# Batch 7's seven products in another order, its u and tail in three rounds, and a tail matrix padded to 128 columns

## The chip, the cores and the metric

The kernel runs on one core of one Trainium2 chip. The metric is the device time of one execution in microseconds (us), the median over the runs shown. TensorE is called PE in the profile, VectorE DVE, ScalarE ACT, GpSimd POOL, and SyncE, which issues most DMAs, SP.

## The reference

Inputs are `q`, `k`, `v` of 8 batches x 8 heads x 576 positions x 64, and four matrices. Each batch passes through a linear attention and then through a mixer:

```python
kv = einsum('bhsf,bhfd->...', phi(k), v)      # phi: relu, times cos and sin of the position
x  = (phi(q) @ kv) / (phi(q) @ z + 1e-6)      # heads side by side: 576 x 512 per batch
h  = x^T @ U @ V                              # U 576 x 32, V 32 x 576
u  = x + h^T
out = u + relu(u @ w_ch1) @ w_ch2             # 512 x 2048 and 2048 x 512
```

## The kernel before, in words

**Tiling.** The 576 positions of a batch are 4 chunks of 128 and a tail of 64. The tails of two batches (2 pr and 2 pr + 1) share one tile of 128 partitions, so there are 8 main parts and 4 paired tails. All products run in bf16 with fp32 sums in PSUM, which has 8 banks: g0, g1, g2, T, o0, o1, and X, which is two banks allocated as one tile.

**The stages of a batch.** k and q are scaled (`k_prep`, `q_prep`), `kv_unit` makes kv, `x_unit` makes x, `A_unit` makes A = (x^T U)^T. `u_mm` (L468) multiplies V by A for the four groups `j` of 128 columns: each is a matmul with only 32 rows of contraction, placed on rows 32 j of the array, once for each of the 4 chunks. `u_add` (L481, DVE) adds x. `u_tail` (L488) does the same for the paired tails: for each j and for each of the two batches i one matmul whose weights `V_tl` have 32 rows and 64 columns, placed at rows 32 j and columns 64 i; the add is at L504. `utr_dma` transposes u by a DMA. `g1_main` (L569) is the first mixer product for the first six batches. For the paired tails it is `g1_tail` (L709). `half_part` (L862) is the second mixer product from batch 2 on, by seven products of half size in place of eight; eight matmuls with 256 columns for each part.

**Batches 6 and 7** also use seven products instead of eight for the first mixer matrix. `g1_cross(b, p, i)` (L651), i from 1 to 7, is a product of two matmuls for block pair p of 0 to 7. Product 1 opens the accumulator X, 6, 7 and 4 are added to it one after the other; product 2 is Y, which lies in the same bank as X; product 5 opens Z in another bank and 3 is added to it. Between these, `g1_join` (L682) reads the partial sums: `P1`, `U2` (copies of X by ACT) and `P5` (a copy of Z by ACT), `C11` (DVE, P1 + Y), `C22` (DVE, P5 + X, and then ACT's relu), `C12` (DVE, U2 + Z; ACT's relu of X, L688; DVE's relu, L698). For batch 7, X and Y lie in g0 and Z in g1 for even p, in g2 and T for odd p.

**The order of the work** is written out by hand. `slots` is a list of main steps; `todo` hangs further work behind a slot (`put`), in the order in which it was put. Every engine executes its instructions in the order in which the program issues them, and waits where a semaphore says so. In the last stage before the end, the slots of batch 7's groups alternate with the 14 half parts of batch 6 (`beside_g`): a group of p is products 1 and 2 of p and 7 of p-1 (`opened`, `third`), then a half part, then products 6 and 5 of p, 3 and 4 of p-1 (`second`, `closed`), then a half part.

`attention_plan` (L1000) sets the slots of u and tails. For batch 7 (w = 189, a_at = 14): `u_mm` of j = 0, 1, 2 behind slot 205, of j = 3 behind 208; `u_tail` of j = 0, 1, 2 behind 212, of j = 3 behind 214. These fall in batch 6's section, whose slots hold `g1_cross` and `g1_join` of batch 6 and the half parts of batch 5. There DVE also makes `w1_sum(4, 0)` (L613, L629), put behind slot 211 by the loop at L1442. `four_banks` (L457) allocates X anew for each of the four steps.

Of the kernel before, what the change touches and what calls it, by code (L numbers as in the profile page):

```python
# [17 lines left out]
def kernel(  # L18
# [27 lines left out]
    def tail(b):  # L46
        lo = TS * (b % 2)
        return slice(lo, lo + TS)
# [78 lines left out]
    def cast(eng, o, i):  # L127
        if eng is nc.scalar:
            nc.scalar.activation(out=o, in_=i, func=AF.Copy, bias=0.0, scale=1.0)  # L129
        else:  # L130
            eng.tensor_copy(out=o, in_=i)  # L131
# [83 lines left out]
    x_tl = const.tile([P, DM], BF16)  # L215
    U_bf = const.tile([P, 6, R], BF16)
    V_bf = const.tile([P, 4, P], BF16)
    V_tl = const.tile([P, TS], BF16)
    A_sb = [const.tile([P, P], BF16, name=f"A_sb{i}") for i in range(4)]
    v_tl = const.tile([P, H, E], BF16)  # L220
    V_.memset(v_tl[:, :, D:E], 1.0)
# [53 lines left out]

    def spread_evac(eng):
        cast(eng, V_bf, v_ps[0].rearrange("r (c p) -> r c p", c=4))
        cast(eng, V_tl, v_ps[1][:, 0:TS])


    k_p, q_p, q_pT, kv_sb, x_bf = {}, {}, {}, {}, {}
# [157 lines left out]
    def A_of(b):  # L439
        return A_sb[b % 4]  # L440
# [27 lines left out]
    def u_mm(b, *spare, js=range(4)):  # L468
        if b not in u_bf:
            u_bf[b] = pool.tile([P, 4, 4, P], BF16, tag="u_bf", bufs=3, name="u_bf")  # L470
        va.setdefault(b, {}).update(zip(js, four_banks(*spare)))
        for c in range(4):
            for j in js:
                rows = slice(j * R, j * R + R)
                nc.tensor.matmul(  # L475
                    out=va[b][j][:, c * P : c * P + P], lhsT=V_bf[rows, c, :],
                    rhs=A_of(b)[rows, :], start=(c == 0), stop=(c == 3),
                    tile_position=(j * R, 0),
                )
# [8 lines left out]
    def u_tail(pr, *spare, js=range(4)):  # L488
        if pr not in u_tl:
            u_tl[pr] = pool.tile(  # L490
                [P, DM], BF16, tag="k_p" if pr == 3 else "u_tl", bufs=1, name="u_tl"
            )
        vt = dict(zip(js, four_banks(*spare)))
        for i in range(2):
            for j in js:
                rows = slice(j * R, j * R + R)
                nc.tensor.matmul(
                    out=vt[j][tail(i), 0:P], lhsT=V_tl[rows, :],
                    rhs=A_of(2 * pr + i)[rows, :], start=True, stop=True,
                    tile_position=(j * R, i * TS),  # L500
                )
        for j in js:
            ns = slice(j * P, j * P + P)
            nc.vector.tensor_tensor(  # L504
                out=u_tl[pr][:, ns], in0=x_tl[:, ns], in1=vt[j][:, 0:P], op=ALU.add
            )

    def uT_alloc(b):
        if b not in uT:
# [100 lines left out]
    def diff(o, x, y, op=ALU.subtract):  # L610
        V_.tensor_tensor(out=o, in0=x, in1=y, op=op)  # L611
# [70 lines left out]
    def g1_join(b, p, i):  # L682

        w, lo, hi = cross[b, p], slice(0, 256), slice(256, 512)
        top, low = hid[b][:, p, :], hid[b][:, p + 8, :]

        def relu(o, x):
            nc.scalar.activation(out=o, in_=x, func=AF.Relu, bias=0.0, scale=1.0)  # L688

        if i == "C11":  # L690
            diff(top[:, lo], w["P1"], w["Y"], ALU.add)
        elif i == "C22":
            diff(low[:, hi], w["P5"], w["X"], ALU.add)
            relu(low[:, hi], low[:, hi])
        elif i == "C12":
            diff(top[:, hi], w["U2"], w["Z"], ALU.add)
            relu(low[:, lo], w["X"])
            V_.tensor_scalar(out=top, in0=top, scalar1=0.0, scalar2=None, op0=ALU.max)  # L698
        else:
            if (b, "kept") not in cross:  # L700
                cross[b, "kept"] = pool.tile(
                    [P, 2, 3, 256], FP32, tag="q_pT" if b == B - 1 else "q_p", bufs=1,
                    name="kept",
                )
            n = ("P1", "U2", "P5").index(i)
            w[i] = cross[b, "kept"][:, p % 2, n]
            cast(A_, w[i], w["Z" if i == "P5" else "X"])
# [292 lines left out]
    def attention_plan(b):  # L1000

        plan = []
        if b < 4:
            w, f_at, q_eng, k_eng, qtr, lo = PLAN[b]
        else:
            w, q_at, k_at, qtr, lo = PLAN[b]

        def put(at, f, *a, tag=False):
            if tag:
                a = a + spare(w + at)  # L1010
            plan.append((w + at, lambda: f(b, *a)))

        for n, c in enumerate(QORD):
            if b > 3:
                put(q_at[0] + q_at[1] * n, q_prep, c, q_at[2:])
                put(k_at[0] + k_at[1] * n, k_prep, c, k_at[2:])
                put(k_at[0] + (3 * n) // 2, v_prep, 0, H, (c,), (G_,))
                continue
            if b == 3:
                q_eng, k_eng = V_ if n == 3 else A_, A_ if n < 3 else None  # L1020
                put((-12, -11, -10, -7, -3)[n], q_prep, c, (q_eng, q_eng))
                put(n - 9 if n < 3 else -5, k_prep, c, (A_, k_eng))
                if n > 2:
                    put(2 * n - 12, k_prep, c, (None, V_))
                put(-4 if n > 2 else -6, v_prep, 0, H, (c,), (A_ if n > 2 else G_,))
                continue
            put(f_at + ((n - 1) % 5 if b == 2 else n), q_prep, c, (q_eng, q_eng))
            put(f_at + 6 + n, k_prep, c, (k_eng, k_eng))
            put((-6, -2, -1, -5, -5)[n], v_prep, 0, H, (c,), (V_ if n > 2 else A_,))
        for n, (c0, c1) in enumerate(((4, 5), (0, 2), (2, 4))):  # L1030
            at = qtr[n] if b > 4 else 1 if b == 3 and n == 2 else qtr + 2 * n
            put(at, qtr_dma, c0, c1)
        plan.append((w + (b == 2), lambda: kv_unit(b, 0, *spare(w), A_ if b > 2 else V_)))
        plan.append((w + 2, lambda: kv_unit(b, 1, *spare(w + 2), A_ if b > 2 else V_)))
        for n, c in enumerate(ORD):
            if b > 3:
                put((3 if b == B - 1 else 4) + 2 * n, x_unit, c, "X", 1)
            elif n % 2:
                put(9 if (b, n) == (3, 3) else 4 + (3 * n) // 2, x_two, c, tag=True)
            else:  # L1040
                put(4 + (3 * n) // 2, x_unit, c, "X", 1)
        a_at = 15 - b if b < 4 else 14
        if b == B - 1:
            put(a_at, A_unit, "s", 1, A_)
        else:
            put(a_at, A_unit, tag=True)
        odd = b % 2 == 1


        def two(at):  # L1050
            return [T1, ("s", 1)] if at >= 88 else [spare(at)] * 2

        if b == B - 1:
            plan.append((w + a_at + 2, lambda: u_mm(b, ("s", 1), js=(0, 1, 2))))
            plan.append((w + a_at + 5, lambda: u_mm(b, js=(3,))))
        else:
            plan.append((w + a_at + 2, lambda: u_mm(b, *two(w + a_at + 2))))
        for j in range(4):
            put(a_at + 2 + j + (2 if b > 4 and j > 1 else 0), u_add, j)
        put(a_at + 3, utr_dma, 0, 2)  # L1060
        put(a_at + (7 if b > 4 else 5), utr_dma, 2, 4)
        if odd:
            if b == B - 1:
                plan.append((w + a_at + 9, lambda: u_tail(b // 2, ("s", 1), js=(0, 1, 2))))
                plan.append((w + a_at + 11, lambda: u_tail(b // 2, js=(3,))))
            else:
                plan.append((w + a_at + 9, lambda: u_tail(b // 2, *two(w + a_at + 9))))
            put(a_at + (11 if b == B - 1 else 10), utr_dma, 4, 5)
        for at, t in zip(lo, loads(b + 1) if lo else ()):
            plan.append((w + at, t))  # L1070
        return plan
# [325 lines left out]
        g1_join(b, p, "P1")  # L1397
        g1_join(b, p, "C11")

    def second(b, p):  # L1400
        g1_cross(b, p, 6)
        g1_cross(b, p, 5)
        g1_join(b, p, "U2")
        g1_join(b, p, "P5")

    def sixth(b, p):
        g1_cross(b, p, 6)
        g1_join(b, p, "U2")
# [5 lines left out]
    def third(b, p):  # L1414
        g1_cross(b, p, 7)
        g1_join(b, p, "C22")

    def closed(b, p):
        g1_cross(b, p, 3)
        g1_cross(b, p, 4)  # L1420
        g1_join(b, p, "C12")

    def crossed(*steps):
        def go():
            for f, b, p in steps:
                f(b, p)

        return go
# [44 lines left out]
    sums(b6, 0, (at, at + 1, at + 6))  # L1473
    sums(b6, 1, (at + 13, at + 15, at + 19))

    def group(p, first, then):
        return crossed(*([(first, b7, p)] if p < 8 else []), *([(then, b7, p - 1)] if p else []))

    groups = [
        group(p, *fs) for p in range(9) for fs in ((opened, third), (second, closed))  # L1480
    ]
    def tail_cross(j):
        if j % 3 == 0:
            t = ps.tile([P, 2, 512], FP32, tag="X", bufs=1, name="gt_ps")[:, 0, :]
# [89 lines left out]
```

## Time and profile before

| what | value |
|---|---|
| runs | 293.47, 294.00, 294.44 us; median 294.0 us |
| the profiled execution | 294.23 us, its span 292.4 us (1.8 us lie around the span) |
| PE clock granted, mean | 0.997 |
| PE busy | 287.0 us, 98% of the span, 2944 matmuls |
| DVE, ACT, POOL busy | 206.7, 169.3, 56.4 us |
| PE matmul of 256 columns, start to start | 0.109 us (0.87 us for 8) |
| stretch 226 to 270 us (batch 7) | PE busy 44.0, DVE 31.8, ACT 26.1 us |

Matmuls are pipelined: a row of the timeline with eight of them shows 1.04 us, but the next matmul can start 0.87 us after the first. So a wait of PE shorter than the pipeline does not show as idle time. It is read from starts: eight matmuls that begin at t end their issue at t + 0.87, and where the next row of PE starts later, that is what it lost.

### The profile page before, as it was taken

Reading aid. Unit: us, or ns where it says so; the run is one execution under the profiler, and the core shown is the slowest. Engines: PE = TensorE matmul, PEld = TensorE weight load, DVE = VectorE, ACT = ScalarE, POOL = GpSimd, SP = SyncE. Lnnn points to the kernel's source line nnn. Section 1 sums busy time; section 2 is a strip of 40 time slices with the busy share of each in tenths; the row PEclk is TensorE's granted clock in tenths of the full one; section 3 lists DMA queues with packets and bytes.
Section 4 is the critical chain, followed back from the end, with each engine's and each line's share of the span. In section 5 each row is a group of like instructions: output and inputs, shape, how many; then the busy total and the mean of one; then the engine's idle time right before and its main releaser. Section 6 shows DMA issues by size and latency. Waiting matters only on the chain.

```text
span 292.4 us, 7343 instructions
## 1 busy us (share of the span) xinstructions
PE 287.0 (98%) x2944; PEld 194.7 (67%) x2944; DVE 206.7 (71%) x503; ACT 169.3 (58%) x353; POOL 56.4 (19%) x92
## 2 busy tenths in 40 slices
PE   8999999999999999999999999999999999999994
PEld 3785564447645545676767666766777888889883
DVE  5968856396876687657547794669968886765773
ACT  2955752177791767578836855497744555567210
POOL 6430500000020002300400501032101223303330
PEclk9999999999999999999999999999999999999998
DMA  7999999999998999999789929992901864336023
GB/s 223 305 254 251 268 151 211 211 331 214 335 196 160 293 242 231 230 328 275 147 216 259 280 66 247 251 302 60 246 4 29 103 143 110 54 92 143 4 103 116
DMA packets 95174, 56.18 MB, mean 192 GB/s; under 512 B 58692, under 2 KB 91844, under 8 KB 95140
## 3 DMA queue, kind: packets, MB, share of 16 engines
q1 hardware_dynamic: 84420, 43.94, 61.6%
q0 software_dynamic: 10528, 11.57, 19.5%
q8 instruction: 23, 0.38, 0.6%
q10 hardware_dynamic: 192, 0.20, 0.2%
q14 instruction: 11, 0.09, 0.2%
HBM read 36.86 MB, written 9.44 MB: 158 GB/s over the span
## 4 chain that ended last, share of the span: by engine, by line
PE 98%; DVE 1%; issue 0%; DVEq 0%
PE g_ps L579 30%; PE h_ps L891 27%; PE o_ps L759 10%; PE c_ps L676 7%; PE gt_ps L719 5%; PE w_ps L234 3%; PE kv_ps L347 3%; PE x_ps L422 3%; PE a_ps L445 1%; PE h_ps L759 1%; PE g_ps L596 1%; PE va_ps L475 1%; PE t_ps L377 1%; PE t_ps L365 1%; PE z_ps L1236 1%; PE kv_ps L1132 0%
## 5 line engine op out<-in xcount | busy, mean ns | idle before, releaser
L579 PE MATMUL g_ps<-uT,w_bf 128*128 128x512 bf16 x402 | 97.3, 379 | 0.0
L588 ACT ACTIVATE hid<-g_ps 128x512 bf16<-128x512 f32 x104 | 61.1, 599 | 57.1 <-PE g_ps L579 56.3
L579 PEld LDWEIGHTS <-w_bf 128*128 128x128 bf16 x402 | 37.5, 98 | 34.4
L891 PEld LDWEIGHTS <-hid 128*128 128x128 bf16 x480 | 45.6, 98 | 9.7
L891 PE MATMUL h_ps<-w_bf,hid 128*128 128x256 bf16 x288 | 37.1, 273 | 0.0
L759 PE MATMUL o_ps<-w_bf,hid 128*128 128x512 bf16 x128 | 30.1, 379 | 0.0
L891 PE MATMUL h_ps<-w_s,S 128*128 128x256 bf16 x208 | 26.5, 272 | 0.0
L131 POOL CAST v_ext<-vst 128x512 bf16<-128x512 f32 (+1 forms) x23 | 14.9, 676 | 59.0 <-DMA vst<-in_v_dram 30.4
L891 PE MATMUL h_ps<-w_s,hid 128*128 128x256 bf16 x192 | 24.9, 273 | 0.0
L847 DVE TENSOR_TENSOR o_sb<-o_sb,h_ps 128x256 f32<-128x256 f32 (+1 forms) x36 | 15.5, 432 | 12.2 <-PE h_ps L891 9.6
L891 PEld LDWEIGHTS <-S 128*128 128x128 bf16 x208 | 20.1, 98 | 4.4
L950 POOL DMA_DIRECT2D out_dram<-o_sb x16 | 9.9, 619 | 65.8 <-DVE o_sb L847 51.4
L483 DVE TENSOR_TENSOR u_bf<-x_bf,va_ps 128x512 bf16<-128x512 bf16 x27 | 17.6, 680 | 6.5 <-PE va_ps L475 2.8
L611 DVE TENSOR_TENSOR hid<-kept,c_ps 128x256 bf16<-128x256 f32 x36 | 14.2, 417 | 10.0 <-ACT kept L129 7.1
L847 DVE TENSOR_TENSOR o_sb<-u_bf,h_ps 128x256 f32<-128x256 bf16 x28 | 11.7, 417 | 13.5 <-PE h_ps L891 13.4
L759 PEld LDWEIGHTS <-hid 128*128 128x128 bf16 x128 | 11.5, 98 | 12.2
L949 POOL DMA_DIRECT2D o_sb<-u_bf x8 | 10.4, 1303 | 32.0 <-DVE rec L413 15.6
L719 PE MATMUL gt_ps<-uT_tl,w_bf 128*128 128x128 bf16 x256 | 16.2, 219 | 0.0
L129 ACT ACTIVATE kept<-c_ps 128x256 f32<-128x256 f32 x36 | 12.5, 380 | 5.9 <-PE c_ps L676 5.6
L432 DVE TENSOR_TENSOR x_bf<-x_ps,rec 128x512 bf16<-128x512 f32 x22 | 15.2, 691 | 0.8
L719 PEld LDWEIGHTS <-w_bf 128*128 128x128 bf16 x256 | 15.1, 98 | 0.7
L306 ACT ACTIVATE k_p<-kst,cosw 128x512 bf16<-128x512 f32 x20 | 14.2, 713 | 0.1
(189 smaller groups left out, 456.6 us busy)
## 6 DMA issues: line engine op xcount, KB each, us to landing
qst<-in_q_dram SPq DMA_DIRECT2D x14, 512.0 KB, 6.2
kst<-in_k_dram SPq DMA_DIRECT2D x14, 512.0 KB, 6.8
vst<-in_v_dram SPq DMA_DIRECT2D x12, 512.0 KB, 6.8
out_dram<-o_sb POOLq DMA_DIRECT2D x19, 256.0 KB, 4.2
out_dram<-o_sb SPq DMA_DIRECT2D x16, 256.0 KB, 2.6
w_bf<-in_moe_w_ch_dram POOLq DMA_DIRECT2D x7, 512.0 KB, 12.3
o_sb<-u_bf POOLq DMA_DIRECT2D x8, 256.0 KB, 3.7
qst<-in_q_dram SPq DMA_DIRECT2D x2, 640.0 KB, 13.5
```

The lines of the kernel that those rows point to most:

```text
L131: eng.tensor_copy(out=o, in_=i)
L306: nc.scalar.activation(out=o, in_=i, func=AF.Relu, bias=0.0, scale=w)
L432: nc.vector.tensor_tensor(out=x_of(b, c, rows).rearrange("p (g i d) -> p g i d", g=2, d=D), in0=view[:, :, :, 0:D], in1=rec[rows].unsqueez ...
L483: nc.vector.tensor_tensor(out=u_bf[b][:, j, :, :], in0=x_bf[b][:, :, ns], in1=va[b][j].rearrange("p (c n) -> p c n", c=4), op=ALU.add,)
L579: nc.tensor.matmul(out=g_ps.rearrange("p (c t) -> p c t", c=4), lhsT=w1_bf[:, d, j * P : j * P + P], rhs=uT[b][:, d, :, :], start=(d == 0) ...
L588: nc.scalar.activation(out=hid[b][:, j, :], in_=g_ps, func=AF.Relu, bias=0.0, scale=1.0)
L611: V_.tensor_tensor(out=o, in0=x, in1=y, op=op)
L676: nc.tensor.matmul(out=w[to].rearrange("p (c t) -> p c t", c=2), lhsT=lhs[:, d, cs], rhs=rhs[:, d], start=(first and d == 0), stop=(d == 1 ...
L719: nc.tensor.matmul(out=g_ps[:, jj, :], lhsT=w1_bf[:, d, j * P : j * P + P], rhs=uT_tl[pr][:, d, :], start=(d == 0), stop=(d == 3),)
L759: nc.tensor.matmul(out=o[:, cols], lhsT=lhs[:, j, c * P : c * P + P], rhs=w2_bf[:, j, cols], start=(j == 0), stop=(j == NJ - 1),)
L847: eng.tensor_tensor(out=o, in0=x, in1=y, op=ALU.add)
L891: nc.tensor.matmul(out=acc, lhsT=lhs[:, j, :], rhs=rhs[:, j, :], start=(j == 0 and at is not None), stop=(j == 7), skip_group_check=at is ...
```

## The change

- **Padding.** `V_tl` becomes 32 rows x 2 x 128 columns per j, zero outside the half that belongs to batch i. Each of the two matmuls of a j now covers all 128 columns at rows 32 j, and the second is added onto the first. A memset (POOL, early) and one copy of 64 columns (POOL, behind `cast_u`) are added.
- **Tail of batches 4 and 5**: `u_tail` moves from behind slot 150 to behind 151, its `utr_dma` by one slot too, which on SP's queue now comes behind a transposing DMA of q.
- **Batch 7's u and tail**: `u_last_mm` (slot 208) does u of j = 3 and, between its matmuls, the tail of j = 0, in X's two banks. The tail's add of j = 0 is put behind slot 211, and `u_tail` of j = 1, 2, 3 behind 212, in place of j = 0, 1, 2. The step behind slot 214 is gone.
- **Batch 7's groups**: first group: 7 of p-1, 1 and 2 of p, C22 of p-1, P1 and C11 of p, relu R22 of p-1. Second group: 3 and 4 of p-1, 6 and 5 of p, relu R21 of p-1, U2 and P5 of p, C12 of p-1. For batch 6 the order stays.

```diff
-    V_tl = const.tile([P, TS], BF16)
+    V_tl = const.tile([P, 2, P], BF16)
+    nc.gpsimd.memset(V_tl, 0.0)
...
-        cast(eng, V_tl, v_ps[1][:, 0:TS])
+        cast(eng, V_tl[:, 0, 0:TS], v_ps[1][:, 0:TS])
+        cast(G_, V_tl[:, 1, TS:P], V_tl[:, 0, 0:TS])
...
+    def u_tail_mm(pr, j, i, t):
+        rows = slice(j * R, j * R + R)
+        nc.tensor.matmul(
+            out=t[:, 0:P], lhsT=V_tl[rows, i, :], rhs=A_of(2 * pr + i)[rows, :],
+            start=(i == 0), stop=(i == 1), tile_position=(j * R, 0),
+        )
...
+    def u_last_mm(b):
+        pr = b // 2
+        u_tl[pr] = pool.tile([P, DM], BF16, tag="k_p", bufs=1, name="u_tl")
+        va[b][3], va[b]["tail"] = four_banks()
+        rows = slice(3 * R, 4 * R)
+        for c in range(4):
+            nc.tensor.matmul(
+                out=va[b][3][:, c * P : c * P + P], lhsT=V_bf[rows, c, :],
+                rhs=A_of(b)[rows, :], start=(c == 0), stop=(c == 3),
+                tile_position=(3 * R, 0),
+            )
+            if c < 2:
+                u_tail_mm(pr, 0, c, va[b]["tail"])
...
-            plan.append((w + a_at + 5, lambda: u_mm(b, js=(3,))))
+            plan.append((w + a_at + 5, lambda: u_last_mm(b)))
...
-                plan.append((w + a_at + 9, lambda: u_tail(b // 2, ("s", 1), js=(0, 1, 2))))
-                plan.append((w + a_at + 11, lambda: u_tail(b // 2, js=(3,))))
+                plan.append((w + a_at + 8, lambda: u_tail_add(b // 2, 0, va[b]["tail"])))
+                plan.append((w + a_at + 9, lambda: u_tail(b // 2, ("s", 1), js=(1, 2, 3))))
             else:
-                plan.append((w + a_at + 9, lambda: u_tail(b // 2, *two(w + a_at + 9))))
-            put(a_at + (11 if b == B - 1 else 10), utr_dma, 4, 5)
+                at = w + a_at + (10 if b == 5 else 9)
+                plan.append((at, lambda at=at: u_tail(b // 2, *two(at))))
+            put(a_at + (11 if b == 5 else 10), utr_dma, 4, 5)
...
-    groups = [
-        group(p, *fs) for p in range(9) for fs in ((opened, third), (second, closed))
-    ]
+    FIRST = ((1, 7), (0, 1), (0, 2), (1, "C22"), (0, "P1"), (0, "C11"), (1, "R22"))
+    THEN = (
+        (1, 3), (1, 4), (0, 6), (0, 5), (1, "R21"), (0, "U2"), (0, "P5"), (1, "C12"),
+    )
+    groups = [in_order(p, *steps) for p in range(9) for steps in (FIRST, THEN)]
```

In `FIRST` and `THEN` a pair is (how many p back, product or join).

More of the change, by code (lines that the diff above doesn't have):

```diff
@@ L495, in u_tail, with u_tail_add @@
             for j in js:
[L496 to L501, printed above, removed]
-        for j in js:
-            ns = slice(j * P, j * P + P)
-            nc.vector.tensor_tensor(
-                out=u_tl[pr][:, ns], in0=x_tl[:, ns], in1=vt[j][:, 0:P], op=ALU.add
-            )
+                u_tail_mm(pr, j, i, vt[j])
+        for j in js:
+            u_tail_add(pr, j, vt[j])
+    def u_tail_mm(pr, j, i, t):
[4 more added lines that the diff above has]
+        )
+    def u_tail_add(pr, j, t):
+        ns = slice(j * P, j * P + P)
+        nc.vector.tensor_tensor(
+            out=u_tl[pr][:, ns], in0=x_tl[:, ns], in1=t[:, 0:P], op=ALU.add
+        )
[9 more added lines that the diff above has]
+                tile_position=(3 * R, 0),
+            )
+            if c < 2:
+                u_tail_mm(pr, 0, c, va[b]["tail"])
     def uT_alloc(b):
@@ L693, in g1_join @@
             diff(low[:, hi], w["P5"], w["X"], ALU.add)
+        elif i == "R22":
             relu(low[:, hi], low[:, hi])
@@ L696, in g1_join @@
             diff(top[:, hi], w["U2"], w["Z"], ALU.add)
+            V_.tensor_scalar(out=top, in0=top, scalar1=0.0, scalar2=None, op0=ALU.max)
+        elif i == "R21":
             relu(low[:, lo], w["X"])
-            V_.tensor_scalar(out=top, in0=top, scalar1=0.0, scalar2=None, op0=ALU.max)
         else:
@@ L1398, in opened @@
         g1_join(b, p, "C11")
[L1400 to L1404, printed above, removed]
     def sixth(b, p):
@@ L1416, in third @@
         g1_join(b, p, "C22")
+        g1_join(b, p, "R22")
     def closed(b, p):
@@ L1420, in closed @@
         g1_cross(b, p, 4)
+        g1_join(b, p, "R21")
         g1_join(b, p, "C12")
@@ L1474, with in_order, go @@
     sums(b6, 1, (at + 13, at + 15, at + 19))
-    def group(p, first, then):
-        return crossed(*([(first, b7, p)] if p < 8 else []), *([(then, b7, p - 1)] if p else []))
-    groups = [
-        group(p, *fs) for p in range(9) for fs in ((opened, third), (second, closed))
-    ]
+    def in_order(p, *steps):
+        def go():
+            for back, i in steps:
+                if 0 <= p - back < 8:
+                    (g1_cross if isinstance(i, int) else g1_join)(b7, p - back, i)
+        return go
+    FIRST = ((1, 7), (0, 1), (0, 2), (1, "C22"), (0, "P1"), (0, "C11"), (1, "R22"))
[3 more added lines that the diff above has]
+    groups = [in_order(p, *steps) for p in range(9) for steps in (FIRST, THEN)]
     def tail_cross(j):
```

## The prediction

> **What bounds the kernel now.** I read the page's busy times and the chain first, then the timeline around each place that the change touches, and last the dependences in the two programs' order.
>
> ```profile
> PE 287.0 (98%) x2944; PEld 194.7 (67%) x2944; DVE 206.7 (71%) x503; ACT 169.3 (58%) x353; POOL 56.4 (19%) x92
> PE 98%; DVE 1%; issue 0%; DVEq 0%
> ```
>
> PE is the bound from end to end, and the change leaves PE's 2944 matmuls in number. So only two things can move the time: matmul blocks that take longer or shorter to issue, and moments at which PE waits. Those waits are short and hidden inside "busy", so I read them from starts: eight matmuls of 256 columns issue in 0.87 us (0.109 each, the chain's pieces "0.87 PE h_ps L891 x8"). The profiled execution took 294.23 us with a span of 292.4; the median is 294.0. I sum against 294.23 and take off the 0.23 at the end.
>
> **Padding alone.** Two tails are only padded. Before, the eight V_tl matmuls at 57.30 and at 109.48 let the next row start 0.20 us later (57.50, 109.68): all eight run side by side. With 128 columns j's second matmul needs the same 32 rows as its first, so there are two rounds of four. The nearest rows are u_mm's, four rounds: 0.34 us (166.78 to 167.12). From 0.20 for one round to 0.34 for four, a round costs about 0.03 to 0.05. I take +0.03 for each tail, +0.06 for two; bounds 0 and +0.1.
>
> **The tail of batches 4 and 5.** The timeline there:
>
> ```profile
> 172.34 1.04 PE L891 MATMUL h_ps<-w_s,hid 128*128 128x256 bf16 x8
> 172.83 0.67 DVE L483 TENSOR_TENSOR u_bf<-x_bf,va_ps 128x512 bf16<-128x512 bf16 x1
> 173.30 0.49 PE L497 MATMUL va_ps<-A_sb,V_tl 32*64 32x128 bf16 x8
> 173.73 1.04 PE L579 MATMUL g_ps<-uT,w_bf 128*128 128x512 bf16 x4
> ```
>
> From its first matmul to the next row the block takes 0.43 us instead of 0.20: its fourth matmul needs the bank that u_add of j = 3 (172.83 to 173.50) still reads. A slot later four matmuls of 512 columns come first (0.86 us by the chain, 0.22 each), from 173.21 to 174.07; u_add is long done. Gain 0.23, less 0.03 for padding: -0.20. The g_ps that moves forward needs ACT's relu of 172.54 to 173.14, in time. DVE's four u_tl adds start about 0.35 later than 174.15; behind them k_p's scaling ends near 175.8, and kv_unit, which reads it, starts at 179.81. The SP swap lets a transpose of q go ahead of the tail's, whose reader comes tens of us later. POOL's memset shifts its start by what a memset of half v_ext's size costs (0.52 for 520 columns: 0.26), against 1.70 us in which POOL then waits for q; its copy falls into the 14.92 us of waiting for k. All nothing.
>
> **Batch 7's u and tail.** Here the change takes away and adds.
>
> ```profile
> 232.80 1.28 DVE L483 TENSOR_TENSOR u_bf<-x_bf,va_ps 128x512 bf16<-128x512 bf16 x2
> 234.00 0.41 DVE L611 TENSOR_TENSOR hid<-kept,c_ps 128x256 bf16<-128x256 f32 x1
> 234.39 0.26 PE L497 MATMUL va_ps<-A_sb,V_tl 32*64 32x128 bf16 x6
> 234.44 0.29 DVE L698 TENSOR_SCALAR hid<-hid 128x512 bf16<-128x512 bf16 x1
> 234.65 0.69 DVE L611 TENSOR_TENSOR w_s<-w_bf,w_s 128x1024 bf16<-128x1024 bf16 x1
> 235.26 0.41 DVE L847 TENSOR_TENSOR o_sb<-o_sb,h_ps 128x256 f32<-128x256 f32 x1
> 235.59 0.68 DVE L504 TENSOR_TENSOR u_tl<-x_tl,va_ps 128x128 bf16<-128x128 bf16 x3
> 236.43 0.24 PE L497 MATMUL va_ps<-A_sb,V_tl 32*64 32x128 bf16 x2
> 236.60 0.39 PE L676 MATMUL c_ps<-uT,w_s 128*128 128x256 bf16 x2
> 236.98 0.38 PE L676 MATMUL c_ps<-uT_s,w_bf 128*128 128x256 bf16 x2
> 237.18 0.28 DVE L504 TENSOR_TENSOR u_tl<-x_tl,va_ps 128x128 bf16<-128x128 bf16 x1
> ```
>
> Gone: the separate block of j = 3. The half part before it starts at 235.46, so its issue ends at 236.33 and the next product starts at 236.60: 0.27. Gone, if DVE is in time: the wait before 236.98, where 0.22 would follow 236.60 and 0.38 does: 0.16 (product 4 waits for C22 behind the three adds at 235.59, ended 236.93).
>
> Added: the two matmuls of the tail's j = 0 between u's four of j = 3. Those use other rows of the array, so they run beside u's: I take 0. No row of before alternates the two weights. The far end is that each of the four alternations costs what entering a tiled block costs, 0.10 (236.33 to 236.43), +0.4; the near end is slightly negative, since u's four on one group of rows wait for one another anyway. The nearest rows are u_mm's, which step from one row group to the next without loss, hence 0. [...] The tail of j = 1, 2, 3 takes two rounds: +0.03.
>
> Added, and decisive: a wait. `four_banks` hands out X, and X now holds j = 0's tail, so the first matmul of `u_tail` for j = 1, 2, 3 waits for j = 0's add. In the program of before it waited only for u_add of j = 3, which ends at 234.08, and PE started at 234.39. In the changed program's order j = 0's add stands on DVE right behind `w1_sum`: both hang on slot 211, and the loop at L1442 put w1_sum first. DVE works without a pause from 228.60 on, so the add starts where w1_sum lets the next one start, 235.26, lasts 0.28 (row 237.18) and ends at 235.54. With 0.05 from a DVE end to PE (236.93 to 236.98) PE starts at 235.6 at the earliest, 235.7 if the weights are loaded only then: a wait of 1.2 to 1.3 us, and PE executes nothing behind it meanwhile. I take +1.2. [...]
>
> What follows shifts by 1.27: products 1 and 2 from 235.84, the half part to 237.59, product 4 at 237.81. C22 then ends near 237.6, so the 0.16 is gone indeed. Sum of the part: 1.2 + 0.03 - 0.27 - 0.16 = +0.80.
>
> **Batch 7's groups.** Two of the waits:
>
> ```profile
> 246.10 1.04 PE L891 MATMUL h_ps<-w_s,S 128*128 128x256 bf16 x8
> 246.66 0.40 ACT L688 ACTIVATE hid<-c_ps 128x256 bf16<-128x256 f32 x1
> 247.10 0.60 PE L676 MATMUL c_ps<-uT,w_bf 128*128 128x256 bf16 x4
> 247.76 1.04 PE L891 MATMUL h_ps<-w_s,hid 128*128 128x256 bf16 x8
> 248.22 0.75 DVE L611 TENSOR_TENSOR hid<-kept,c_ps 128x256 bf16<-128x256 f32 x2 [1.39 <-ACT kept L129]
> 248.69 0.60 PE L676 MATMUL c_ps<-uT_s,w_s 128*128 128x256 bf16 x4
> ```
>
> 246.10 + 0.87 is 246.97; product 1 of the next p starts at 247.10, because ACT's relu of X, third in ACT's order behind U2 and P5, ends at 247.06. 247.76 + 0.87 is 248.63; product 6 starts at 248.69, because C11 (same bank) has just ended. Read in this way from 244 to 266 PE loses 0.14, 0.13, 0.06, 0.06, 0.13, 0.06, 0.06, 0.13, 0.06, 0.04: 0.86 in ten places.
>
> In the new order, with time 0 at product 7: 7 at 0, 1 and 2 from 0.22, half part 0.65, 3 at 1.53, 4 at 1.74, 6 at 1.96, 5 at 2.18, half part 2.40, next 7 at 3.27. Results reach ACT or DVE about 0.30 after the last matmul's start (243.90 to 244.20). Product 6 needs C11: product 2's last starts at 0.55, P1 runs 0.85 to 1.23, C11 to 1.67; 0.29 spare. Product 4 needs C22: at most 1.1 behind an add of the last half part; 0.6 spare. Product 1 needs the relu of X a whole half part and a product earlier. The new wait is product 7 on U2: the half part's copy holds ACT to 2.1, R21 to 2.5, U2 to 2.9; 3.27 is due, 0.3 spare. Only p = 1, where a sum of 0.68 runs ahead on DVE (244.16), stays late: C22 to 245.18, C11 to 245.52, product 6 due at 245.53, 0.04. So -0.82; bounds -0.86 and 0.
>
> **Sum.** 0.06 - 0.20 + 0.80 - 0.82 = -0.16: 294.23 becomes 294.07, and the median 294.0 becomes 293.9 (rounded). About 0.3%, 0.9 us, is what a measurement of this kernel can tell from no change, so this is no change.
>
> **Rivals.** (1) Faster: the wait on j = 0's tail add does not appear, because the add comes early enough or the bank is free. It takes 1.2 out, leaves the 0.16 in, and gives 292.8. For it: DVE is busy but not PE-bound there, and a DVE that runs 0.6 earlier halves the wait. Against it: the order of the program and the unbroken row of DVE work. (2) Slower: ACT decides batch 7's groups. R22, which waits for DVE, a half part's copy and R21 (0.38 to 0.42 each) now stand on ACT ahead of U2, which product 7 waits for. If C22 holds R22 back so far that U2 ends over 0.3 later in each p, product 7 loses what product 1 lost, 0.13 to 0.2 for 8 values of p, on top of the 0.06 at product 6 if C11 is late by the same: about +0.2 instead of -0.82, so 294.9; it ends beyond 0.9 us where alternating weights cost 0.1 or more as well: 295.0. For it: ACT's rows from 240 to 273 leave no pause over 0.96 us. Against it: 0.3 spare. (3) The reordering does not do what it says: waits move from products 1 and 6 to 3, 4 or 7 at the same total. Then -0.82 is 0, and the result 294.7.
>
> **How the numbers follow.** Forecast 0.62, (1) 0.17, (2) 0.14, (3) 0.07. Faster by over 0.3% is (1): 0.17. Slower is (2) and 0.02 each of (3) and of the forecast, where alternating weights cost 0.4 and the waits of the groups stay in part: 0.18. The rest, 0.65 (0.60 of the forecast, 0.05 of (3)), is within. The range takes in (1), with the 0.1 by which padding is uncertain, and (2): 292.7 to 295.0.
>
> **What would show it.** In the changed profile: the V_tl block of j = 1, 2, 3 starts about 1.2 after the half part before it has issued, just behind the u_tl add that follows w1_sum; from 244 to 266 products start 0.87 after their half parts; the tail of batches 4 and 5 takes 0.23; the two other tails 0.23. The prediction is wrong if PE is not held at batch 7's tail, or if product 7 starts late behind ACT's copy.

## The result and the profile after

The changed kernel takes 294.85 us (median of 22 runs, 293.91 to 296.51) against 293.9 for the kernel before (22 runs, 293.19 to 295.04): ratio 1.0032, 95% interval 1.0019 to 1.0045. It is slower by 0.9 us, where no change was forecast. Its profiled execution took 295.05 us with a span of 293.3, that of the kernel before 294.23 and 292.4. The ratios here and below leave out three executions that were slow at a lower granted clock: one of the kernel before (299.62 us, 0.983) and two of gap_staging's twelve (299.98 and 299.51 us, 0.993 and 0.991; without them its median is 295.14).

The page of the changed kernel (34 matmul records are missing in this trace, so its 2910 are no change in the work):

```profile
PE 284.0 (97%) x2910; PEld 194.6 (66%) x2944; DVE 207.9 (71%) x503; ACT 169.2 (58%) x353; POOL 58.0 (20%) x94
...
q1 hardware_dynamic: 84420, 43.94, 64.8%
...
PE 77%; DMA 7%; DVE 6%; SPq 4%; ACT 3%; issue 2%; POOL 0%; POOLq 0%; DVEq 0%; ACTq 0%
```

Before, the chain was PE to 98%; now DMAs hold 7% of it. The same queue in the page of before moved the same packets (second column) and bytes in a smaller share of the engines' time:

```profile
q1 hardware_dynamic: 84420, 43.94, 61.6%
```

Over 16 engines that is 0.616 x 16 x 292.4 us / 84420 = 34.1 ns a packet before and 36.0 ns after. The chain of the changed kernel from 55 to 95 us (start, us, what) shows where it reaches PE:

```profile
58.23 6.95 DMA vst<-in_v_dram
65.18 0.63 ACT v_ext L129
65.81 0.49 ACT hid L610
66.34 3.61 PE g_ps L601 x16
...
79.62 7.82 DMA vst<-in_v_dram
...
88.24 0.62 POOL v_ext L131
...
88.90 0.78 PE kv_ps L349 x19
```

The loads of v for batches 2 and 3 land so late that PE waits behind the casts of them. In the kernel before, the chain of this window has PE rows alone.

Both traces have all 2944 weight loads, in the same order but for single blocks. Set against each other one by one, they give the shift: how much later the changed kernel is at each place, counted from the first load of each (between batch 7's last u and its tail the changed kernel has made two loads more, so there the count is moved by two).

| place, us in the kernel before | shift, us | step | forecast |
|---|---|---|---|
| 41 to 57 | -0.15 | | |
| behind the padded tail at 57 | -0.12 | +0.03 | +0.03 |
| 66 to 88, in three steps (0.31, 0.37, 0.52) | +1.08 | +1.20 | 0 |
| behind the padded tail at 109 | +1.11 | +0.03 | +0.03 |
| behind the tail of batches 4 and 5 | +0.91 | -0.20 | -0.20 |
| before batch 7's last u | +0.92 | +0.01 | |
| behind it, with j = 0's tail in it | +0.92 | 0.00 | 0 |
| behind the tail of j = 1, 2, 3 | +2.16 | +1.24 | +1.23 |
| behind product 4, with the block of j = 3 gone | +1.73 | -0.43 | -0.43 |
| the end, behind batch 7's groups | +0.93 | -0.80 | -0.82 |

So in this execution every place that the prediction priced came out within 0.02 us of its price, -0.13 together against its -0.16, and 1.2 us came in at places where it had nothing.

Those places, in the timeline of the changed kernel. The tail of batches 4 and 5:

```profile
174.33 0.67 DVE L485 TENSOR_TENSOR u_bf<-x_bf,va_ps 128x512 bf16<-128x512 bf16 x1
...
175.29 0.29 PE L504 MATMUL va_ps<-A_sb,V_tl 32*128 32x128 bf16 x8
...
175.51 0.72 PE L915 MATMUL h_ps<-w_bf,hid 128*128 128x256 bf16 x5
```

u_add of j = 3 is done by 175.00, ahead of the block, and holds nothing; the block takes 0.22 instead of 0.43. Batch 7's tail:

```profile
234.34 1.04 PE L915 MATMUL h_ps<-w_s,hid 128*128 128x256 bf16 x8
...
235.58 0.69 DVE L633 TENSOR_TENSOR w_s<-w_bf,w_s 128x1024 bf16<-128x1024 bf16 x1
236.18 0.28 DVE L511 TENSOR_TENSOR u_tl<-x_tl,va_ps 128x128 bf16<-128x128 bf16 x1
...
236.52 0.29 PE L504 MATMUL va_ps<-A_sb,V_tl 32*128 32x128 bf16 x6 [1.14 <-DVE u_tl L511]
...
238.49 0.38 PE L698 MATMUL c_ps<-uT,w_s 128*128 128x256 bf16 x2
...
238.71 0.38 PE L698 MATMUL c_ps<-uT_s,w_bf 128*128 128x256 bf16 x2
```

The half part has issued at 235.21; the tail starts at 236.52, behind the add that stands behind w1_sum. Product 4 follows product 3 after 0.22 (238.49 to 238.71), where it was 0.38. In the groups products start 0.87 or 0.88 after their half part; the ten waits are gone:

```profile
245.96 1.04 PE L915 MATMUL h_ps<-w_s,S 128*128 128x256 bf16 x8
...
246.83 0.38 PE L698 MATMUL c_ps<-uT,w_s 128*128 128x256 bf16 x2
...
247.73 1.04 PE L915 MATMUL h_ps<-w_s,S 128*128 128x256 bf16 x8
...
248.60 0.38 PE L698 MATMUL c_ps<-uT_s,w_s 128*128 128x256 bf16 x2
```

### The profile page after: what moved, and what is told of

It is laid out like the page before. It is cut to its first block, busy times and chain, and to the rows that moved or that the text cites. A ratio compares the mean times of both kernels' runs of the same rounds, so it can differ in the third digit from the quotient of the medians.

```text
span 293.3 us, 7321 instructions
## 1 busy us (share of the span) xinstructions
PE 284.0 (97%) x2910; PEld 194.6 (66%) x2944; DVE 207.9 (71%) x503; ACT 169.2 (58%) x353; POOL 58.0 (20%) x94
## 3 DMA queue, kind: packets, MB, share of 16 engines
q1 hardware_dynamic: 84420, 43.94, 64.8%
## 4 chain that ended last, share of the span: by engine, by line
PE 77%; DMA 7%; DVE 6%; SPq 4%; ACT 3%; issue 2%; POOL 0%; POOLq 0%; DVEq 0%; ACTq 0%
PE h_ps L915 26%; PE g_ps L601 24%; PE c_ps L698 6%; DMA vst<-in_v_dram 5%; PE gt_ps L743 5%; PE o_ps L783 4%; PE kv_ps L349 3%; PE x_ps L424 2%; DMA qst<-in_q_dram 2%; SPq L107 2%; DVE u_bf L485 2%; PE h_ps L783 1%; PE a_ps L447 1%; SPq L91 1%; SPq L543 1%
## 5 line engine op out<-in xcount | busy, mean ns | idle before, releaser
L601 PE MATMUL g_ps<-uT,w_bf 128*128 128x512 bf16 x378 | 95.5, 379 | 1.3
L610 ACT ACTIVATE hid<-g_ps 128x512 bf16<-128x512 f32 x104 | 61.0, 599 | 56.8 <-PE g_ps L601 56.1
L783 PE MATMUL o_ps<-w_bf,hid 128*128 128x512 bf16 x122 | 29.4, 379 | 0.4 <-issue 0.2
L131 POOL CAST v_ext<-vst 128x512 bf16<-128x512 f32 (+1 forms) x23 | 15.9, 718 | 66.6 <-DMA vst<-in_v_dram 66.6
```

The costliest lines, as they stand in the source:

```text
L601: nc.tensor.matmul(out=g_ps.rearrange("p (c t) -> p c t", c=4), lhsT=w1_bf[:, d, j * P : j * P + P], rhs=uT[b][:, d, :, :], start=(d == 0) ...
L610: nc.scalar.activation(out=hid[b][:, j, :], in_=g_ps, func=AF.Relu, bias=0.0, scale=1.0)
L783: nc.tensor.matmul(out=o[:, cols], lhsT=lhs[:, j, c * P : c * P + P], rhs=w2_bf[:, j, cols], start=(j == 0), stop=(j == NJ - 1),)
```

## The experiments

Each was timed in five rounds beside the kernel before on the same chip; its median there was 293.93, 293.96 and 293.88 us in the three groups of four. A ratio is the one on record, with its 95% interval; it differs from the quotient of the medians printed here by up to 0.15%.

**First four: which part of the change costs, and which gains.** Theory A put the late loads down to POOL's added work at the start; theory B held that this work has nothing to do with them, and so forecast no loss for padding alone.

*pads_only*, the kernel before with V_tl padded alone:

```
-    V_tl = const.tile([P, TS], BF16)
+    V_tl = const.tile([P, 2, P], BF16)
+    nc.gpsimd.memset(V_tl, 0.0)
...
+        cast(G_, V_tl[:, 1, TS:P], V_tl[:, 0, 0:TS])
... u_tail: lhsT=V_tl[rows, i, :], out 128 columns, start=(i == 0), stop=(i == 1)
```

> The kernel before with V_tl padded alone (zeroing and copy on POOL at the start, 128-wide tail matmuls in all four tails); batch 7's order and blocks as before. Theory A (POOL's added work at the start makes the loads of batches 2 and 3 land later, and PE then waits some 1.1 us between 66 and 90 us): +1.1 and +0.1 for padding, 295.0 against 293.9, and the profile shows kv_unit or the g_ps row at 66 to 90 us late behind a vst load. Theory B (those waits have nothing to do with POOL's work at the start): +0.1, no difference, 293.9 to 294.0.

Measured: 295.49 us, 1.0064 (1.0039 to 1.0089), queue q1 at 65.4%. The loss comes with the padding, against theory B's forecast.

*pool_late*, the changed kernel with the zeroing and the copy behind the w2 loads:

```
-    nc.gpsimd.memset(V_tl, 0.0)
-        cast(G_, V_tl[:, 1, TS:P], V_tl[:, 0, 0:TS])
         w2_load(j0, j1)
+    G_.memset(V_tl[:, 0, TS:P], 0.0)
+    G_.memset(V_tl[:, 1, 0:TS], 0.0)
+    cast(G_, V_tl[:, 1, TS:P], V_tl[:, 0, 0:TS])
```

> The changed kernel with V_tl's zeroing and copy moved on POOL from the start to behind the w2 loads (about 33 us), so that POOL's start is that of the kernel before. Theory A: the 1.1 us between 66 and 90 us go, 293.8 against 294.85 for the changed kernel, level with the kernel before. Theory B: stays at 294.8 or so, 0.9 over the kernel before, with the waits at 66 to 90 us in its profile.

Measured: 294.77 us, 1.0032 (1.0012 to 1.0051), q1 at 65.7%, waits for vst at 66 and 88 us as in the changed kernel. Theory A falls: it is padding, but not its work on POOL.

*groups_only*, the kernel before with FIRST and THEN alone:

```
-    groups = [group(p, *fs) for p in range(9) for fs in ((opened, third), (second, closed))]
+    groups = [in_order(p, *steps) for p in range(9) for steps in (FIRST, THEN)]
... R22 and R21 as steps of their own
```

> The kernel before with batch 7's groups in the new order alone (FIRST and THEN, with the two relus on ACT as steps of their own). Both theories: the ten waits of PE from 244 to 266 us go from 0.86 to about 0.04 us, so 0.8 less: 293.1 against 293.9 (0.997). If the waits only move to other products, 293.9.

Measured: 293.09 us, 0.9981 (0.9964 to 0.9997). Set against those of the kernel before, its weight loads gain 0.80 us between batch 7's first group and the end. As both expected.

*add_early*, the changed kernel with one line moved:

```
-                plan.append((w + a_at + 8, lambda: u_tail_add(b // 2, 0, va[b]["tail"])))
+                plan.append((w + a_at + 7, lambda: u_tail_add(b // 2, 0, va[b]["tail"])))
```

> The changed kernel with the u_tl add of batch 7's j = 0 one slot earlier, so that on DVE it stands ahead of w1_sum. Both theories: PE's wait of 1.2 us ahead of the tail of j = 1, 2, 3 goes; up to 0.2 of it comes back as product 4's wait for C22. 1.0 to 1.2 under the changed kernel: 293.7 to 293.9, level with the kernel before. If a wait for something else takes its place, 294.8.

Measured: 294.35 us, 1.0012 (0.9994 to 1.0029): 0.5 under the changed kernel's median, half of what was expected; the two intervals overlap, so it is the trace that shows where the gain goes. The wait at the tail is gone (236.47, 0.10 after the half part before it has issued), and another took half its place. The timeline behind it:

```profile
237.87 0.68 DVE L511 TENSOR_TENSOR u_tl<-x_tl,va_ps 128x128 bf16<-128x128 bf16 x3
238.45 0.38 PE L698 MATMUL c_ps<-uT,w_s 128*128 128x256 bf16 x2
238.46 0.75 DVE L633 TENSOR_TENSOR hid<-kept,c_ps 128x256 bf16<-128x256 f32 x2
...
239.26 0.38 PE L698 MATMUL c_ps<-uT_s,w_bf 128*128 128x256 bf16 x2 [0.43 <-DVE hid L633]
```

Product 4 waits for C22 (238.46), which stands on DVE behind the three adds of j = 1, 2, 3: 0.81 after product 3 instead of 0.22, so 0.59. By the weight loads the tail's step is 0.03 instead of 1.24, a gain of 1.21, and 0.59 of it is lost again here.

**Second four: the place in SBUF.** Queue q1 is near 65% in all kernels with the padded tile and near 62% in groups_only, though bytes and packets are the same. What padding changes beside its work is where tiles lie: V_tl grows from 128 to 512 bytes a partition, and every tile allocated behind it lies 384 bytes further on. Before, the staging tiles of q, k and v, and q_p, q_pT, x_bf, uT, u_bf and hid, begin at multiples of 256 bytes (qst at 83200, u_bf at 198144); after, at odd multiples of 128 (83584, 198528). Theory C is that DMA packets take longer there. An unused tile tests this with no work added:

```
     V_tl = const.tile([P, TS], BF16)
+    gap = const.tile([P, 192], BF16)        # 384 bytes; 128 and 64 columns in the two others
```

*before_gap384*:

> The kernel before with an unused tile of 384 bytes a partition behind V_tl, no work added: every tile behind it (the staging tiles of q, k and v, q_p, x_bf, uT, u_bf) lies 384 bytes further on, as in the changed kernel. Theory C (place in SBUF: DMA packets take longer there, and PE waits for the loads of batches 2 and 3): about +1.1, 295.0 against 293.9, queue q1 near 65% of the engines' span instead of 61.6%, packets of 256 bytes at 26 ns instead of 23. Rival (padding's work, not its place): 293.9, 61.6%, 23 ns.

Measured: 295.47 us, 1.0051 (1.0028 to 1.0074). From its page:

```profile
q1 hardware_dynamic: 84420, 43.94, 65.7%
...
PE 85%; DMA 4%; DVE 3%; ACT 3%; SPq 2%; issue 1%; DVEq 0%; ACTq 0%
```

*before_gap256*:

> The same with an unused tile of 256 bytes: the staging tiles come to multiples of 512 bytes, uT and u_bf to odd multiples of 256. Theory C, if multiples of 256 are what counts: 293.9, q1 near 62%. If multiples of 512 count for uT and u_bf: about 295, q1 near 65%. Rival: 293.9.

Measured: 293.77 us, 0.9984 (0.9962 to 1.0006). With the tiles at multiples of 256 again, nothing is lost that can be told. From its page:

```profile
q1 hardware_dynamic: 84420, 43.94, 61.5%
```

*before_gap128*:

> The same with an unused tile of 128 bytes: every tile behind it at an odd multiple of 128. Theory C: about 295.0, q1 near 65%, as with 384. Rival: 293.9, 61.6%.

Measured: 295.27 us, 1.0045 (1.0020 to 1.0069), q1 at 66.0%. So an unused tile of 384 or 128 bytes costs at least about as much as the whole change, and one of 256 bytes nothing that can be told. The place is the cause.

The engines' own instructions are no slower there: in before, before_gap256, before_gap384 and before_gap128 alike the median is 597 or 598 ns for ACT's relu of g_ps, 679 or 680 ns for DVE's u_bf sum, and 379 ns for a matmul of 512 columns. What changes is the time of DMA packets, as the table further down shows.

*vtl192*, the changed kernel with a V_tl that moves the tiles behind it by 256 bytes instead of 384:

```
-    V_tl = const.tile([P, 2, P], BF16)
+    V_tl = const.tile([P, 3 * TS], BF16)
-        cast(eng, V_tl[:, 0, 0:TS], v_ps[1][:, 0:TS])
-        cast(G_, V_tl[:, 1, TS:P], V_tl[:, 0, 0:TS])
+        cast(eng, V_tl[:, TS:P], v_ps[1][:, 0:TS])
... u_tail_mm: lhsT=V_tl[rows, TS - i * TS : 3 * TS - i * TS]
```

> The changed kernel with V_tl as 192 columns (64 of zeros, V's 64, 64 of zeros; the two weights are overlapping views of 128 columns), which is 256 bytes more than before instead of 384 and needs no copy on POOL. Theory C with multiples of 256: 1.1 less than the changed kernel, 293.7 to 293.8, q1 near 62%. If POOL's or TensorE's work of padding were the cause: 294.8, q1 near 62% or 65%.

Measured: 294.07 us, 1.0001 (0.9978 to 1.0024), q1 at 60.3%. With the place put right, the change is what was forecast: no change. The page's chain alone would not have told this: the profiled execution of vtl192, at 295.12 us a long one, has DMA 7% in it too.

**Last four: which tiles, and a better version.**

*gap_staging* and *gap_rest*:

```
         for name in ("qst", "kst", "vst")
     ]
+    gap2 = pool.tile([P, 64], BF16, tag="gap2", bufs=1, name="gap2")    # both kernels
...
     V_tl = const.tile([P, TS], BF16)
+    gap = const.tile([P, 64], BF16)                                     # gap_staging alone
```

> The kernel before with two unused tiles of 128 bytes, one behind V_tl and one behind the staging tiles: q's, k's and v's staging tiles (and A_sb, v_tl) lie 128 bytes further on, at odd multiples of 128, all tiles behind them at multiples of 256 as before. Theory C1 (it is the loads into the staging tiles that take longer): 295.2, nearly the whole loss. Theory C2 (it is the transposes between q_p, q_pT, u_bf and uT, packets of 256 bytes, which take the engines' time from the loads): 293.9, packets of 256 bytes at 23 to 24 ns. Both in part: 294.5.

> The kernel before with one unused tile of 128 bytes behind the staging tiles: these stay where they are, and q_p, q_pT, x_bf, uT, u_bf, hid and the rest lie at odd multiples of 128. Theory C1: 293.9, no loss. Theory C2: 295.2, packets of 256 bytes at 26 ns, and those of 1024 bytes into the staging tiles at 52 to 54 as in the kernel before. Both in part: 294.5.

Measured: 295.26 us, 1.0032 (1.0011 to 1.0054), and 294.79 us, 1.0027 (1.0006 to 1.0048). Each interval lies above 1, so both cost in part; how much of the loss is whose stays open, for the intervals overlap. In gap_rest's one profiled execution PE lost only 0.15 us between 30 and 90 us, so where its loss arises is not shown. Mean duration of single packets, in ns, from the traces' records of them:

| kernel | staging off 256 | rest off 256 | 256 bytes, q1 | 512 bytes, q0 | 1024 bytes, q1 | ratio |
|---|---|---|---|---|---|---|
| before | no | no | 23.4 | 55.2 | 53.7 | 1 |
| before_gap256 | no | no | 24.2 | 55.5 | 52.4 | 0.9984 |
| vtl192 | no | no | 23.6 | 55.3 | 52.2 | 1.0001 |
| gap_staging | yes | no | 24.4 | 55.5 | 56.2 | 1.0032 |
| gap_rest | no | yes | 25.7 | 64.0 | 52.5 | 1.0027 |
| before_gap384 | yes | yes | 25.8 | 64.0 | 57.5 | 1.0051 |
| before_gap128 | yes | yes | 26.7 | 64.0 | 56.1 | 1.0045 |
| changed | yes | yes | 26.0 | 64.1 | 55.2 | 1.0032 |

Packets of 1024 bytes, mostly the loads into the staging tiles, go with the place of these; those of 256 and 512 bytes with the place of the rest. That slower packets are what makes the loads late is the reading that fits; no run slowed the packets alone.

*vtl192_early* is vtl192 with the line of add_early:

> The changed kernel with V_tl in 192 columns (no tile moved to an odd multiple of 128) and j = 0's tail add ahead of w1_sum. Theory C and the sum of waits: 0.8 less than the changed kernel for the place, 0.5 for the add: 293.4 to 293.6. If the two gains do not add, 294.0.

Measured: 293.17 us, 0.9976 (0.9961 to 0.9991). The two gains add: their sum gave 293.5, within the interval.

*best* lets C22 and C11 go ahead of the three adds as well:

```
-                plan.append((w + a_at + 9, lambda: u_tail(b // 2, ("s", 1), js=(1, 2, 3))))
+                plan.append((w + a_at + 9, lambda: va[b].update(
+                    rest=u_tail(b // 2, ("s", 1), js=(1, 2, 3), add=False))))
+                plan.append((w + a_at + 10, lambda: u_tail_adds(b // 2, va[b]["rest"])))
... the transpose of this tail follows them, at a_at + 11
```

> The same, and the three u_tl adds of j = 1, 2, 3 a slot later, so that on DVE C22 and C11 stand ahead of them, and product 4, which waited 0.6 us for C22 when only the first add was moved, finds it done. 0.4 to 0.6 less than with the first add moved alone: 292.9 to 293.1, faster than the kernel before by 0.8 to 1.0. If another wait takes its place: 293.5.

Measured: 292.71 us, 0.9959 (0.9939 to 0.9978): 1.2 us under the kernel before and 2.1 under the changed kernel's median. Its timeline:

```profile
235.69 0.74 DVE L638 TENSOR_TENSOR hid<-kept,c_ps 128x256 bf16<-128x256 f32 x2
236.27 0.38 PE L703 MATMUL c_ps<-uT,w_s 128*128 128x256 bf16 x2
236.35 0.67 DVE L516 TENSOR_TENSOR u_tl<-x_tl,va_ps 128x128 bf16<-128x128 bf16 x3
236.49 0.38 PE L703 MATMUL c_ps<-uT_s,w_bf 128*128 128x256 bf16 x2
```

Product 4 starts 0.22 after product 3. The interval overlaps that of vtl192_early; by the weight loads the step at product 4 is 0.59 lower in best, as expected.

## Why the prediction was wrong

**The step that failed** is "All nothing", the sentence that closes the part on the tail of batches 4 and 5 and prices what the padding does away from TensorE. It weighed the instructions that padding adds, two on POOL, and these do cost nothing that can be seen: pool_late takes them out of the start and stays where the changed kernel is. What it did not ask is what a larger tile moves. The same tile allocation without any work (before_gap384) is 1.5 us slower in the median. No rival held it either: the causes of a loss that were weighed were ACT, alternating weights and waits that move. That 294.85 still lies within 292.7 to 295.0 is luck: the upper end was set by rival (2), ACT deciding the groups, which did not come.

The page of before had the sign of risk in its DMA row (mean busy share of the 16 engines, in tenths, for 40 slices of 7.3 us):

```profile
DMA  7999999999998999999789929992901864336023
```

It is 9 from the second slice to the twenty-third but for three digits (8, 7, 8), some 160 us. That packets which take some per cent longer (36.0 ns on q1 instead of 34.1) make loads land later where the engines have so little time to spare is, as said above, the reading that fits; the prediction took the loads as given. The chain of before, 98% PE, hid that: a chain names what ended last, not what ended shortly before.

Of the distances tried, 256 bytes costs nothing that can be told (0.9984), 128 and 384 do (1.0045 and 1.0051). Packets of 256 bytes took 26.0 ns in the changed kernel instead of 23.4, and those of 1024 bytes, mostly the loads that write into the staging tiles, 56.2 ns in gap_staging against 53.7 in before. Why a packet takes longer at an odd multiple of 128 is not shown.

**Padding on TensorE**, +0.06: it came as forecast. The times cannot tell it, for pads_only (1.0064) and before_gap384 (1.0051) have overlapping intervals, but the weight loads can: in all seven traces with padded weights the shift grows by 0.03 at each of the tails at 57 and 109 us, and in the six other kernels by 0.00.

**The tail of batches 4 and 5**, -0.20: its block went from 0.43 to 0.22, and the shift fell by 0.20 there, as forecast. The gain depends on the execution, which the prediction did not say: in the trace of groups_only the unmoved tail did not wait at all (0.20 from 173.29 to 173.49). Where the staging tiles lie off 256 the step is worth more: in before_gap128 the unmoved tail waits 0.61 us for u_add of j = 3, in before_gap384 0.41, in pads_only 0.39. So moving it takes back part of what the place costs, which may be why the changed kernel (1.0032) lies under before_gap384 (1.0051).

**Batch 7's u and tail**, +0.80: +0.81 by the shifts. The wait came where and as long as written: 1.2 and 0.03 for the two rounds were forecast, the shift there is 1.24 (the row, which counts from the end of the half part before, shows 1.14). It hangs on w1_sum, as add_early shows by taking the add out from behind it. In both kernels VectorE ran the two in the program's order: in the changed kernel w1_sum from 235.58 and the add from 236.18, in add_early the add from 236.08 and w1_sum from 236.93. The alternating weights cost nothing: the shift is 0.92 before their block and 0.92 behind it, so the 0 taken for them held and the far end, +0.4, fell.

**Batch 7's groups**, -0.82: -0.80 by the shifts in the changed kernel and in groups_only, whose ratio is 0.9981. Rival (2), ACT deciding the groups, did not come, and rival (3), waits that only move, did not either.

**Rival (1)**, no wait at the tail, was priced at 1.2 us and more; add_early, which makes it true, gained 0.5. The prediction had noted that 0.16 of a wait for C22 comes back; 0.59 came. C22 queues behind the three adds, and the earlier PE gets to product 4, the longer it waits there.

**The sums** hold but for roundings: 294.07 less 0.23 is 293.8 and not 293.9, and the ten waits add up to 0.87.

## What to carry to other kernels

Count what a change allocates, not only what it runs: where transfers fill a stage, see that every tile a DMA writes or reads keeps its place modulo 256 bytes (128 or 384 bytes further cost 1.3 and 1.5 us here, 256 nothing that can be told), and test a suspicion with an unused tile of the same size, which moves everything and does nothing. A chain that is all PE says nothing of how close the loads are behind; look at the DMA row for that. A wait taken away can show the next one in the same queue (in add_early 0.59 of the 1.21 us gained was lost again behind the three adds), so move all of the block that stands ahead of the critical instruction, as the last version did.

## What the runs showed of the hardware

In the eight kernels of the table above, DMA packets to or from SBUF tiles that begin at odd multiples of 128 bytes took longer than at multiples of 256: 25.7 to 26.7 ns instead of 23.4 to 24.4 for 256 bytes, 64.0 to 64.1 instead of 55.2 to 55.5 for 512 bytes on queue q0, 55.2 to 57.5 instead of 52.2 to 53.7 for 1024 bytes.

How late loads reached PE varied from execution to execution: between 30 and 90 us the profiled executions of the six kernels with all those tiles off 256 lost 0.6 to 2.4 us against that of the kernel before, those of the five others with them on it 0 to 0.6. The two ranges touch (pads_only and groups_only both lost 0.56), so one profiled execution does not tell the two apart; medians of many runs and the packets' durations do.

VectorE's bf16 sums of 1024 columns into hid took 0.67 to 0.69 us in all 279 cases of the fourteen traces in which POOL was idle, and up to 1.11 us beside a cast or a sum on POOL (49 of 57 over 0.70). Late loads bring POOL's casts of v beside these sums, which is how the tail of batches 4 and 5 came to wait in before_gap128:

```profile
168.80 3.21 POOL L131 CAST v_ext<-vst 128x512 bf16<-128x512 f32 x4 [2.35 <-DMA vst<-in_v_dram]
170.44 1.09 DVE L834 TENSOR_TENSOR hid<-hid 128x1024 bf16<-128x1024 bf16 x1
```

Why a sum takes longer beside POOL's work is not shown.
